# Four feed-forward blocks computed ahead instead of five, in a gated linear-attention and SwiGLU kernel, with GpSimd products, masked states by bank and another product order in two units

## The chip, the cores and the metric

The kernel runs on one core of a Trainium2 chip. The core has a matrix engine (TensorE, PE in the profile, with its weight loads shown apart as PEld), a vector engine (VectorE, DVE), a scalar engine (ScalarE, ACT), a general engine (GpSimd, POOL) and a queue engine (SyncE, SP) that here only issues transfers. The metric is the device time of one execution in microseconds (us); before the change the median of three runs is 1647.71 us (1643.01 to 1648.73).

## The reference

`x` is 2048 rows of 576. It is normalised (layer norm without weights), and two branches read the result: linear attention with 32 heads of 18, and a SwiGLU feed-forward network with 4608 hidden columns. The output is `x + s * silu(ffn)`.

```python
def _A_ref(x, wqkv, w_phi, wo):
    qkv = (x @ wqkv).reshape(B, S, 3, H, Dh)              # q, k, v by head
    pq = jnp.einsum("bhsd,hdf->bhsf", q, w_phi)           # pk likewise
    phi_q = concat([softmax(pq), softmax(-pq)])           # phi_k likewise: 36 features a head
    kv = jnp.einsum("bhsf,bhsd->bhfd", phi_k, v)
    z  = jnp.einsum("bhsf->bhf", phi_k)
    num = jnp.einsum("bhqf,bhfd->bhqd", phi_q, kv)
    den = jnp.einsum("bhqf,bhf->bhq", phi_q, z)[..., None] + 1e-6
    return (num / den).reshape(B, S, D) @ wo
def _B_ref(x, w_gate, w_up, w_down):
    return (silu(x @ w_gate) * (x @ w_up)) @ w_down
```

## The kernel before

Every float32 operand of a large product is split into a high and a low part, and three products (high by high, high by low, low by high) are added in PSUM. The rows of `x`, normalised and transposed, lie in eight tiles `X00` to `X13`: two row halves, four column blocks of 128 plus a packed remainder.

**Order of the program.** First a preparation (norm, folding of `w_phi` into the key and query weights), then the key stage, which adds up the 36 by 18 state of each head and the key sums in the PSUM tiles `kvp`. At its end the states are masked to block diagonals and split into `KVH` and `KVL`, and the key sums go through `zc` and two small products into `zb`, where every partition holds all of them. Then comes the query stage, then the feed-forward stage, twice over the 36 blocks of 128 hidden columns: once per row half.

**Query stage.** It goes over 16 row tiles (`q_tile`), in eight pairs. A tile is 28 matmuls of 288 columns into the PSUM tile `p2` (one buffer), two maxima and subtractions on VectorE, two exponentials on ScalarE into `e`, a sum per head (`sm`), the product of `e` with the key sums (`ez`), its sum per head (`y`), reciprocals, and the scaling of `e`. For each pair `numer` transposes `e` (`pt`), splits it (`ph`, `pl`), multiplies by the states (`po`), splits again (`oh`, `ol`), and `project` multiplies by the output weights and copies out (`so`).

**Blocks ahead.** While the query stage waits for VectorE and ScalarE, TensorE works on the first EARLY feed-forward blocks in the plain way (`early_tile`): for each row half two tiles, each 14 matmuls of 512 columns for the gate and 14 for the up projection, into two PSUM banks `pe`. ScalarE takes the SiLU, VectorE multiplies, and the result `h` goes to `h_dram`. The last such block (EARLY - 1) is written behind the query stage: its first row half, then the loads of the operand tiles of the feed-forward stage (`operands`, the sums of `x` blocks that the key stage stored in `sum_dram`), then its second row half.

**Feed-forward stage.** A block that was not computed ahead is a unit of `gate_up`: gate and up for 1024 rows by a Winograd form of Strassen's product, seven products of seven matmuls of 512 columns in the PSUM tiles `px` (two buffers), `py` and `pw`, with ScalarE copies (`snap`) and VectorE additions between them. Its weights (`gate_up_weights`) are loaded (`ld`), combined on GpSimd (`ts`, `ld`), split (`w`), and stored in `w_dram` for the second row half. A block that was computed ahead is a unit of `stored`, which only loads `h`. The products with `w_down` run from a queue whose items `fill` puts between the products of `gate_up`; they write `pd`. `tails` prepares the remainder rows of the weights for four blocks at a time and stores them in `t_dram`.

**What sets the order.** Source order and priorities go through a scheduler that fixes the order on each engine ahead of time; `issue_after` adds an order on one engine without a wait. On the chip each engine takes its instructions in that order, and each queue its transfers: an instruction that waits holds up all behind it on its engine.

## Time and profile before

| | |
|---|---|
| median of three runs | 1647.71 us (1643.01 to 1648.73) |
| the profiled execution | 1645.38 us, span 1643.6 us |
| granted TensorE clock, mean | 0.998 |
| preparation and key stage | 0 to about 230.5 us |
| query stage, up to its first transposes | 230.5 to 271 us |
| query stage, the rest | 271 to 488 us |
| last block ahead | 488 to 512.7 us |
| feed-forward stage | 512.7 us to the end |

A busy time is the sum of an engine's instructions. Rows of a group read: line, engine, operation, tiles (out<-in), shapes, count, then busy time in us and mean length in ns of one, then the idle time of the engine just before them and what ended it. A row of the timeline reads: start, length, engine, line, operation, tiles, count, and in brackets the idle time before and who ended it. The ends of matmuls are modelled and overlap, so the pace of a run of matmuls is taken from the chain of waits, where a piece is start, length and count.

### The profile page before, as it was taken

Reading aid. Unit: us, or ns where it says so; the run is one execution under the profiler, and the core shown is the slowest. Engines: PE = TensorE matmul, PEld = TensorE weight load, DVE = VectorE, ACT = ScalarE, POOL = GpSimd, SP = SyncE. Lnnn points to the kernel's source line nnn. Section 1 sums busy time; section 2 is a strip of 40 time slices with the busy share of each in tenths; the row PEclk is TensorE's granted clock in tenths of the full one; section 3 lists DMA queues with packets and bytes.
Section 4 is the critical chain, followed back from the end, with each engine's and each line's share of the span. In section 5 each row is a group of like instructions: output and inputs, shape, how many; then the busy total and the mean of one; then the engine's idle time right before and its main releaser. Section 6 shows DMA issues by size and latency. Waiting matters only on the chain.

```text
span 1643.6 us, 25222 instructions
## 1 busy us (share of the span) xinstructions
PE 1606.3 (98%) x9385; PEld 1428.2 (87%) x9385; DVE 1173.2 (71%) x1733; ACT 723.1 (44%) x1407; POOL 655.0 (40%) x699
## 2 busy tenths in 40 slices
PE   6999999999999999999999999999999999999997
PEld 5899987999987788888888888888888888888886
DVE  7667768989862678788777788825566766666578
ACT  5533344454432554454444444445433433333334
POOL 3385661433213455355445365313243324133132
PEclk9999999999999999999999999999999999999999
DMA  9522243433239545555545554685454655555445
GB/s 293 197 79 78 88 133 114 119 109 110 79 108 329 183 162 172 182 171 177 174 167 181 178 176 156 222 299 157 134 159 138 199 183 172 168 180 182 139 114 173
DMA packets 121741, 268.47 MB, mean 163 GB/s; under 512 B 12786, under 2 KB 53362, under 8 KB 119826
## 3 DMA queue, kind: packets, MB, share of 16 engines
q1 hardware_dynamic: 106652, 246.49, 45.8%
q0 software_dynamic: 3072, 11.02, 2.5%
q10 hardware_dynamic: 11894, 9.35, 1.8%
q8 instruction: 74, 1.21, 0.3%
q14 instruction: 49, 0.40, 0.1%
HBM read 167.19 MB, written 99.61 MB: 162 GB/s over the span
## 4 chain that ended last, share of the span: by engine, by line
PE 66%; DVE 2%; DMA 1%; issue 1%; POOL 0%; ACT 0%; SPq 0%; DVEq 0%; ACTq 0%
PE pd L805 24%; PE px L706 24%; PE pw L706 12%; PE py L706 6%; PE pe L92 1%; DVE acc L777 0%; DVE w L59 0%; DMA rb<-in_B_w_down 0%; DMA ld<-in_B_w_gu 0%; DVE hh L59 0%; DMA X<-s_dram 0%; DVE dw L59 0%; DVE ha L766 0%; DVE acc L778 0%; DVE s L740 0%
## 5 line engine op out<-in xcount | busy, mean ns | idle before, releaser
L805 PEld LDWEIGHTS pd<-dw,hh 128*128 128x128 f32 x3048 | 433.6, 189 | 25.5 <-DVE dw L59 2.0
L805 PE MATMUL pd<-dw,hh 128*128 128x288 f32 x3048 | 449.7, 297 | 3.2 <-DVE dw L59 1.5
L706 PE MATMUL px<-X,w 128*128 128x512 f32 x1488 | 385.9, 393 | 2.1 <-ACT w L58 1.3
L706 PEld LDWEIGHTS px<-X,w 128*128 128x128 f32 x1488 | 270.2, 188 | 55.5 <-ACT s L735 4.0
L706 PE MATMUL pw<-X,w 128*128 128x512 f32 x744 | 191.8, 393 | 0.0
L706 PEld LDWEIGHTS pw<-X,w 128*128 128x128 f32 x744 | 139.1, 188 | 31.2 <-DVE s L740 0.3
L740 DVE TENSOR_TENSOR s<-pw,s 128x512 f32<-128x512 f32 x124 | 85.3, 688 | 103.2 <-ACT s L735 91.7
L930 DVE TENSOR_TENSOR acc<-pd,acc 128x576 f32<-128x576 f32 x128 | 96.3, 753 | 85.3 <-PE pd L805 85.1
L735 ACT COPY s<-px 128x512 f32<-128x512 f32 x124 | 72.6, 586 | 160.0 <-PE px L706 159.9
L92 PE MATMUL pe<-X,wh 128*128 128x512 f32 (+1 forms) x380 | 121.4, 401 | 5.3 <-ACT h L119 2.2
L58 ACT CAST hh<-ha 128x512 fp32r<-128x512 f32 x140 | 82.7, 619 | 92.9 <-PE pd L805 72.6
L59 DVE TENSOR_TENSOR hh<-ha,hh 128x512 fp32r<-128x512 f32 x140 | 109.9, 811 | 18.1 <-ACT hh L58 17.1
L902 POOL TENSOR_TENSOR hb<-hb 128x512 f32<-128x512 f32 x34 | 46.7, 1372 | 161.9 <-DVE hb L762 161.5
L59 DVE TENSOR_TENSOR w<-ld,w 128x512 fp32r<-128x512 f32 (+1 forms) x93 | 79.6, 858 | 37.6 <-ACT w L58 36.3
L706 PE MATMUL py<-X,w 128*128 128x512 f32 x372 | 97.7, 396 | 1.1 <-ACT py L747 1.1
L706 PE MATMUL px<-X,wt 96*128 96x512 f32 x248 | 97.9, 395 | 0.0
L915 POOL TENSOR_TENSOR ha<-ha 128x512 f32<-128x512 f32 x34 | 52.6, 1563 | 104.0 <-DVE hh L59 104.0
L889 POOL TENSOR_TENSOR h<-ha,hb 128x512 f32<-128x512 f32 x34 | 44.9, 1321 | 123.2 <-DVE ha L766 90.1
L58 ACT CAST w<-ld 128x512 fp32r<-128x512 f32 (+1 forms) x93 | 50.9, 549 | 90.1 <-POOL ld L696 58.0
L92 PEld LDWEIGHTS pe<-X,wh 128*128 128x128 f32 (+1 forms) x380 | 69.9, 189 | 20.6 <-DVE h L122 3.4
L693 POOL TENSOR_TENSOR ts<-ld 128x256 f32<-128x256 f32 x31 | 27.3, 880 | 140.7 <-issue 70.0
L747 ACT COPY py<-px 128x512 f32<-128x512 f32 x62 | 35.5, 572 | 103.7 <-PE px L706 84.4
(262 smaller groups left out, 3238.1 us busy)
## 6 DMA issues: line engine op xcount, KB each, us to landing
w_dram<-w SPq DMA_DIRECT2D x90, 512.0 KB, 2.9
w<-w_dram SPq DMA_DIRECT2D x90, 512.0 KB, 4.5
wt<-t_dram SPq DMA_DIRECT2D x61, 336.0 KB, 3.6
ld<-in_B_w_gu SPq DMA_DIRECT2D x31, 512.0 KB, 4.5
X<-sum_dram SPq DMA_DIRECT2D x8, 1280.0 KB, 11.4
rt<-in_B_w_down SPq DMA_DIRECT2D x33, 288.0 KB, 3.0
rb<-in_B_w_down SPq DMA_DIRECT2D x33, 288.0 KB, 4.3
w_dram<-w SPq DMA_DIRECT2D x30, 256.0 KB, 2.2
```

The source lines that it names most:

```text
L58: nc.scalar.copy(hi, src)
L59: nc.vector.tensor_sub(lo, src, hi)
L92: last = nc.tensor.matmul(ps, l, r, start=n == 0, stop=n == len(pairs) - 1)
L706: nc.tensor.matmul(ps, l, r, start=first and n == 0, stop=last and n == len(mm) - 1, skip_group_check=True)
L735: nc.scalar.copy(t, ps)
L740: nc.vector.tensor_add(t, ps, t)
L747: nc.scalar.copy(yp, xp)
L805: nc.tensor.matmul(ps, l, r, start=first and n == 0 and m == 0, stop=n == len(hs) - 1 and m == 2, skip_group_check=True)
L889: sub(s, g["h"][0][0], g["h"][0][1])
L902: nc.gpsimd.tensor_add(a21, a21, g["h"][1][1])
L915: sub(a12, a12, g["h"][0][0])
L930: nc.vector.tensor_add(a2, pd[:, :, 0:HALF], a2)
```

## The change

- EARLY is 4: the plain way takes four blocks, and `gate_up` 32 units in each row half instead of 31. TAILS stays 8.
- Each row tile's product with the key sums moves from VectorE (one of 1152 elements) to GpSimd (two of 576), each with its own sum on VectorE. The buffer `ez` becomes two of half the size.
- In `tails` the subtraction of 896 elements moves from VectorE to GpSimd, and eight of the twelve stores from the GpSimd queue to SP. Both groups of GpSimd instructions are put behind the key-sum products of given row tiles.
- Masking and splitting of the states go by PSUM bank (three steps instead of ten), the key sums are copied out by bank, and `zb` is filled by two copies instead of four.
- In the first two units of `gate_up` the products run in another order, the one with S4 into a free `pd` bank, and no `fill` is called. `operands` loads in a matching order.
- The last `so` copies get high priority.

```diff
-EARLY = 5
+EARLY = 4
...
-            for i in range(3):
-                for j in range(4 if i < 2 else 2):
-                    w = GROUPS[(4 * i + j) // 2][1]
-                    nc.scalar.copy(zc[0:w, 4 * i + j:4 * i + j + 1], kvp[i][0:w, j, w:w + 1])
...
+            banks = [(i, 4 if i < 2 else 2, GROUPS[2 * i][1]) for i in range(3)]
+            for i, n, w in banks:
+                nc.scalar.copy(zc[0:w, 4 * i:4 * i + n], kvp[i][0:w, 0:n, w])
...
+            nc.scalar.copy(z2[:, :, 0:o], zp[:, :, 0:o])
+            nc.scalar.copy(z2[:, :, o:D], zq[:, 0:2 * (D - o)].rearrange("p (s n) -> p s n", s=2))
+            for i, n, w in banks:
+                km = qc.tile([GW, 4, GW], F32, name="km")
+                nc.vector.tensor_mul(km[0:w, 0:n, 0:w], kvp[i][0:w, 0:n, 0:w],
+                                     m4[0:w, 0:w].unsqueeze(1).to_broadcast([w, n, w]))
+                split(KVH[0:w, 4 * i:4 * i + n, 0:w], KVL[0:w, 4 * i:4 * i + n, 0:w], km[0:w, 0:n, 0:w])
...
-            def tails(n):
+            def tails(n, k):
...
+                with tc.issue_after(sums_z[2 * k + 1].ins):
+                    sub(t[:, 4], t[:, 2], t[:, 0])
...
                 nc.scalar.copy(hi, t)
-                nc.vector.tensor_sub(t, t, hi)
...
-                        nc.gpsimd.dma_start(t_dram[n, q, b], src[32 * q:32 * q + 32])
+                with tc.issue_after(sums_z[2 * k + 3].ins):
+                    sub(t, t, hi)
+                    for b, src in enumerate((hi.bitcast(F32), hi.bitcast(F32), t)):
+                        for q in range(4):
+                            (nc.sync, nc.sync, nc.gpsimd)[b].dma_start(t_dram[n, q, b], src[32 * q:32 * q + 32])
...
-                ez = qk.tile([P, 2 * D], F32, name="ez", bufs=1)
-                nc.vector.tensor_mul(ez, e, zb)
...
-                nc.vector.reduce_sum(y, heads(ez), axis=AX.X)
+                for s in range(2):
+                    ez = qk.tile([P, D], F32, name="ez", bufs=2)
+                    sums_z.append(nc.gpsimd.tensor_mul(ez, e[:, s * D:(s + 1) * D], zb[:, s * D:(s + 1) * D]))
+                    nc.vector.reduce_sum(y[:, s * H:(s + 1) * H], heads(ez), axis=AX.X)
...
-                        nc.scalar.copy(so, ps[:, 0:HALF])
+                        with tc.high_priority() if last else ExitStack():
+                            nc.scalar.copy(so, ps[:, 0:HALF])
...
-        for n in (0, 6, 1, 3, 5, 2, 4):
+        for n in (0, 6, 3, 1, 5, 4, 2):
...
         product(wp, w, 4, S1, True, False)
+        if opening < 2:
+            product(xp, w, 5, S2, False, False)
+            s2 = snap(xp)
+            product(yp, w, 1, A12, False, True)
+            silu_y()
+            product(xp, w, 2, S3, False, False)
+            s3 = snap(xp)
+            add(wp, s3)
+            add(wp, s2)
+            zp = fps.tile([P, 2, 512], F32, name="pd", bufs=2)[:, 0]
+            product(zp, w, 3, S4, True, True)
+            add(zp, s2)
+            top(s2)
+            product(xp, w, 6, A22, False, True)
+            silu_x(s3)
+            return h
```

Three places show how it moves instructions. The first is SP's queue at the end of the query stage, where `X` are the operand tiles of the feed-forward stage, `ld` and `wt` its first weights and `h` results of the last block ahead. Before:

```order
L675 DMA ld<-in_B_w_gu 128x4x256
L691 DMA wt<-t_dram 96x896
L686 DMA w_dram<-w_5380 128x1024
L686 DMA w_dram<-w_5389 128x1024
L686 DMA w_dram<-w_5393 128x1024
L998 DMA acc<-in_B_w_down 128x576 x2
L123 DMA h_dram<-h 128x512
L662 DMA X_5302<-sum_dram 128x2560
L662 DMA X_5300<-sum_dram 128x2560
L123 DMA h_dram<-h 128x512
L662 DMA X_5304<-sum_dram 128x2560
L662 DMA X_5306<-sum_dram 128x2560
```

and with the change:

```order
L123 DMA h_dram<-h 128x512
L664 DMA X_5161<-sum_dram 128x2560
L664 DMA X_5165<-sum_dram 128x2560
L123 DMA h_dram<-h 128x512
L664 DMA X_5163<-sum_dram 128x2560
L664 DMA X_5159<-sum_dram 128x2560
L123 DMA h_dram<-h 128x512
L677 DMA ld<-in_B_w_gu 128x4x256
L693 DMA wt<-t_dram 96x896
L677 DMA ld<-in_B_w_gu 128x4x256
```

The four operand tiles now stand ahead of the first weights, and the weights behind two more results `h`.

The second place is TensorE at the entry of the feed-forward stage; `X_60`, `X_61` and `X_63` are rows of `x`, the others of the sums, and a new `w` number is another weight tile. Before:

```order
L744 MATMUL py<-X_60,w_5380 128x512
L706 MATMUL px<-X_60,w_5380 128x512 x6
L706 MATMUL px<-X_60,wt 128x512
L706 MATMUL pw<-X_5300,w_5389 128x512 x6
L706 MATMUL pw<-X_5300,wt 128x512
L706 MATMUL py<-X_61,w_5380 128x512 x6
L706 MATMUL py<-X_61,wt 128x512
L706 MATMUL px<-X_5302,w_5389 128x512 x6
L706 MATMUL px<-X_5302,wt 128x512
L706 MATMUL px<-X_60,w_5413 128x512 x5
L706 MATMUL px<-X_5304,w_5393 128x512 x6
L706 MATMUL px<-X_5304,wt 128x512
```

and with the change:

```order
L746 MATMUL py<-X_60,w_5239 128x512
L708 MATMUL px<-X_60,w_5239 128x512 x6
L708 MATMUL px<-X_60,wt 128x512
L708 MATMUL pw<-X_5159,w_5248 128x512 x6
L708 MATMUL pw<-X_5159,wt 128x512
L708 MATMUL px<-X_5161,w_5248 128x512 x6
L708 MATMUL px<-X_5161,wt 128x512
L708 MATMUL py<-X_61,w_5239 128x512 x6
L708 MATMUL py<-X_61,wt 128x512
L708 MATMUL px<-X_5163,w_5252 128x512 x6
L708 MATMUL px<-X_5163,wt 128x512
L708 MATMUL pd<-X_5165,w_5252 128x512 x6
```

Between two products into `px` there now stands one into `pw`, `py` or `pd`; before, `px` followed `px`, and the next unit's first product was cut up to stand between.

The third place is GpSimd in the query stage. Before, it prepared the remainder rows (`tl`, `th`) and issued their stores:

```order
L555 DMA t_dram<-th 32x896 x8
L555 DMA t_dram<-tl 32x896 x4
L555 DMA t_dram<-th 32x896 x8
L555 DMA t_dram<-tl 32x896 x4
L547 TENSOR_TENSOR tl<-tl 128x128
L548 TENSOR_TENSOR tl<-tl 128x128
L549 TENSOR_TENSOR tl<-tl 128x128
L550 TENSOR_TENSOR tl<-tl 128x128
```

and with the change:

```order
L571 TENSOR_TENSOR ez<-e,zb 128x576 x2
L553 TENSOR_TENSOR tl<-tl,th 128x896
L547 TENSOR_TENSOR tl<-tl 128x128
L556 DMA t_dram<-tl 32x896 x4
L548 TENSOR_TENSOR tl<-tl 128x128
L549 TENSOR_TENSOR tl<-tl 128x128
L550 TENSOR_TENSOR tl<-tl 128x128
L571 TENSOR_TENSOR ez<-e,zb 128x576 x2
L553 TENSOR_TENSOR tl<-tl,th 128x896
L556 DMA t_dram<-tl 32x896 x4
```

The products `ez` stand between the parts of the remainder rows, and the stores of `th` have gone to SP.

On TensorE, the matmuls into `pe` from the first query tile on stood as 104 ahead of the first transposes, 212 from there to the last output projection, and 104 behind it; with the change they stand as 61, 198 and 49.

More of the change, by code (lines that the diff above doesn't have):

```diff
@@ L510, in gated_hedgehog_kernel @@
-            for i in range(2 * NG):
-                o, w = GROUPS[i // 2]
-                km = qc.tile([GW, GW], F32, name="km", bufs=2)
-                nc.vector.tensor_mul(km[0:w, 0:w], kvp[i // 4][0:w, i % 4, 0:w],
-                                     mask.rearrange("p h d -> p (h d)")[0:w, 0:w])
-                split(KVH[0:w, i, 0:w], KVL[0:w, i, 0:w], km[0:w, 0:w])
+            zc = qc.tile([GW, 12], F32, name="zc")
+            m4 = mask.rearrange("p h d -> p (h d)")
+            banks = [(i, 4 if i < 2 else 2, GROUPS[2 * i][1]) for i in range(3)]
@@ new lines, in gated_hedgehog_kernel @@
+            for i, n, w in banks:
+                nc.scalar.copy(zc[0:w, 4 * i:4 * i + n], kvp[i][0:w, 0:n, w])
+            zp, zq = kps.tile([P, 2, 512], F32, name="p2"), kps.tile([P, 512], F32, name="vw")
+            for g, (o, w) in enumerate(GROUPS):
+                for s in range(2):
+                    d = zp[:, s, o:o + w] if g < NG - 1 else zq[:, s * w:s * w + w]
+                    nc.tensor.matmul(d, zc[0:w, 2 * g + s:2 * g + s + 1].to_broadcast([w, P]), ident[0:w, 0:w],
+                                     start=True, stop=True)
@@ L576, in q_tile @@
                                      den.unsqueeze(1).to_broadcast([P, 2, H]))
-                last_e.append(nc.vector.tensor_mul(heads(e), heads(e), spread(r, 2 * H)))
+                nc.vector.tensor_mul(heads(e), heads(e), spread(r, 2 * H))
                 return e
```

50 lines of the change are left out of this document (22 added, 28 removed).

## The prediction

> **What bounds the kernel now.** I read the page's engine shares and chain first, then the chain's pieces for the pace of matmuls, then the stretches around the query stage.
>
> ```profile
> PE 1606.3 (98%) x9385; PEld 1428.2 (87%) x9385; DVE 1173.2 (71%) x1733; ACT 723.1 (44%) x1407; POOL 655.0 (40%) x699
> PE 66%; DVE 2%; DMA 1%; issue 1%; POOL 0%; ACT 0%; SPq 0%; DVEq 0%; ACTq 0%
> ```
>
> TensorE is busy 98% of the span, and the chain runs through it: time is won by fewer matmuls, or where TensorE still waits. Pieces of the chain give the pace:
>
> ```profile
> 496.22 16.63 PE pe L92 x70
> 1017.33 3.22 PE pd L805 x24
> 1125.09 1.63 PE py L706 x7
> ```
>
> A matmul of 512 columns costs 237.6 ns in a plain block (16.63 / 70) and 232.9 ns in a unit (1.63 / 7), one of 288 columns 134 ns. The stretches (length, then busy time and count of PE, PEld, DVE, ACT, POOL, then granted clock, DMA share, GB/s) and, below them, the same for instructions on `pe` (there PE, PEld, DVE, ACT):
>
> ```profile
> 230.50:271.00 40.50, 36.32 (x189) 30.58 (x189) 30.80 (x52) 21.06 (x30) 15.76 (x24) 1.00 0.49 154
> 271.00:488.00 217.00, 215.66 (x1457) 196.41 (x1458) 185.68 (x288) 95.01 (x169) 58.58 (x116) 1.00 0.33 98
> 488.00:512.70 24.70, 24.61 (x107) 19.53 (x106) 5.73 (x8) 5.40 (x11) 6.42 (x8) 1.00 0.92 341
> 512.70:552.00 39.30, 35.19 (x143) 26.77 (x142) 19.93 (x26) 15.54 (x31) 16.37 (x17) 0.96 0.68 231
> ...
> 271.00:488.00 217.00, 61.36 (x213) 37.01 (x214) 5.54 (x8) 4.19 (x7) 1.00 0.33 98
> ```
>
> From 271 to 488 us TensorE idles 1.3 us while VectorE is 86% busy: the plain blocks fill what the query stage leaves open. TensorE idles 4.2 us at the stage's start and 4.1 us at the feed-forward entry. Who ended these waits (total, times, longest):
>
> ```profile
> PE pe L92 <- ACT h L119: 2.2, 2, 1.3
> PE pe L92 <- DVE h L122: 2.0, 2, 1.7
> PE pd L805 <- DVE dw L59: 1.5, 1, 1.5
> PE px L706 <- ACT w L58: 1.3, 2, 0.8
> PE p L614 <- ACT so L618: 1.3, 1, 1.3
> PE pt L588 <- DVE e L577: 1.3, 1, 1.3
> PE p L92 <- ACT zb L509: 1.1, 1, 1.1
> PE py L706 <- ACT py L747: 1.1, 2, 0.6
> PE px L706 <- ACT s L735: 0.7, 2, 0.5
> ```
>
> **The exchange of a block.** A plain block is 2 row halves x 2 tiles x 28 = 112 matmuls: 112 x 0.2376 = 26.6 us less. Two units are 2 x 7 x 7 = 98: 98 x 0.2329 = 22.8 us more, as the stage behind 552 us has TensorE full. Net -3.8 us, if what the block covered stays covered. It goes from three places: 43 matmuls (10.2 us) ahead of the first transposes, 14 (3.3 us) in the stage's body, 55 (13.1 us) behind it.
>
> **The stage's body.** TensorE's work there falls to 217.0 - 1.3 - 3.3 = 212.4 us, so VectorE must stay below that. What leaves and stays on it:
>
> ```profile
> L577 DVE TENSOR_TENSOR e<-e,sm 128x1152 f32<-128x1152 f32 x15 | 20.3, 1355 | 0.3
> L278 DVE TENSOR_REDUCE m<-p 128x32 f32<-128x576 f32 x27 | 19.9, 738 | 0.2 <-PE p L92 0.2
> L285 DVE TENSOR_REDUCE sm<-e 128x64 f32<-128x1152 f32 x14 | 18.9, 1347 | 3.8 <-ACT e L282 3.8
> L568 DVE TENSOR_TENSOR ez<-e,zb 128x1152 f32<-128x1152 f32 x14 | 18.6, 1328 | 0.0
> L570 DVE TENSOR_REDUCE y<-ez 128x64 f32<-128x1152 f32 x14 | 18.4, 1317 | 0.0
> ...
> L552 DVE TENSOR_TENSOR tl<-tl,th 128x896 f32<-128x896 f32 x8 | 8.6, 1080 | 0.0
> ```
>
> The key-sum products (18.6) and remainder subtractions (8.6) go; two half sums for one cost 14 x (2 x 0.738 - 1.317) = 2.2: 185.7 - 18.6 - 8.6 + 2.2 = 160.7 us. GpSimd at work slows VectorE where it reads two tiles from SBUF; the key stage shows that, with GpSimd's own price under contention:
>
> ```profile
> L409 DVE TENSOR_TENSOR phi<-phi,sm 128x1152 f32<-128x1152 f32 x14 | 21.7, 1548 | 0.5
> ...
> L328 POOL TENSOR_TENSOR slo<-sraw,shi 128x512 fp32r<-128x512 f32 x14 | 25.2, 1797 | 1.1
> ...
> L889 POOL TENSOR_TENSOR h<-ha,hb 128x512 f32<-128x512 f32 x34 | 44.9, 1321 | 123.2 <-DVE ha L766 90.1
> L555 POOL DMA_DIRECT2D t_dram<-tl x32 | 15.8, 499 | 82.1 <-DVE tl L552 41.8 <-DVE y L571 40.2
> ```
>
> 1548 against 1355 ns adds 15 x 0.19 = 2.9 us: VectorE has 164 of 212 us, 48 to spare, 3.0 us a row tile. A product of 576 costs GpSimd 1.49 to 2.02 us (1321 and 1797 x 576 / 512); I take 1.6. It starts behind the first exponential, so the first half sum finds it done behind VectorE's 1.35 us sum, and the second waits under 1 us: inside the 3.0. GpSimd's own load (32 x 1.6 = 51 us, subtractions 8 x 2.5, 32 stores of 0.5) is under half the stage. The body costs nothing more; queued behind a waiting half sum stand the next tile's maxima and the splits of `numer`, covered by `pe`.
>
> **The stage's start.** `zb` is filled by two copies instead of four with up to four splits between, so the 1.1 us wait falls to some 0.4: -0.7 (0 to -1.1). With 61 instead of 104 matmuls ahead of the transposes, TensorE asks for them after 84 x 0.134 + 61 x 0.2376 = 25.7 us instead of 36.0. The third row tile cannot start before VectorE has subtracted the second tile's maxima (one buffer `p2`), and VectorE's row now puts two half sums, a reciprocal and a split between them. Following that row with the lengths above, I find the third tile 2.7 us late and the transposes 0.7: 3.4 us of waits against 4.2, so -0.8 (-4.2 if all go, +4.2 if they double).
>
> **The last copies.** The 1.3 us wait for `so` had a weight cast ahead of the copy, held up by its load:
>
> ```profile
> 484.91 0.62 ACT L58 CAST w<-ld 128x512 fp32r<-128x512 f32 x1 [3.39 <-DMA ld<-in_B_w_gu]
> 485.43 0.39 ACT L618 COPY so<-p 128x288 f32<-128x288 f32 x1
> 488.37 0.40 ACT L618 COPY so<-p 128x288 f32<-128x288 f32 x1 [2.55 <-DMA s_dram<-so]
> 489.40 0.62 ACT L58 CAST w<-ts 128x512 fp32r<-128x512 f32 x1 [0.64 <-ACT so L618]
> ...
> 495.14 0.42 DVE L59 TENSOR_TENSOR w<-ld,w 128x256 fp32r<-128x256 f32 x1 [1.76 <-ACT w L58]
> 495.48 0.68 DVE L122 TENSOR_TENSOR h<-pe,h 128x512 f32<-128x512 f32 x1
> ```
>
> The copy now stands ahead of that cast: -1.3 (0 to -1.3).
>
> **Behind the stage.** 49 matmuls, 11.6 us, must cover what 104 covered. The last block's `h` stands on VectorE behind the split of the second unit's last weight tile; the last two rows above show it, 10.6 us after the first weights landed. Some 2.5 us of that the cast of `ts` stood behind the `so` copies, which now come first. So 8.1 us remain, with `h` itself 8.8, and TensorE can issue 35 matmuls (8.3 us) before it needs that bank: it waits 0.5 us longer than the first weights land behind the stage's last matmul. In SP's queue:
>
> ```profile
> 479.72 0.58 SPq L675 DMA_DIRECT2D ld<-in_B_w_gu  x1
> ...
> 496.61 3.49 SPq L662 DMA_DIRECT2D X<-sum_dram  x2
> ...
> X<-sum_dram SPq DMA_DIRECT2D x8, 1280.0 KB, 11.4
> ```
>
> They were issued 8.3 us before that matmul (488.0) and landed 5.2 us later. Now two operand tiles stand ahead of them, free some 9 us before the end: 2.6 MB at 341 GB/s take 7.7 us, then the weights 2.5: landed 1.2 us behind the end, so +1.7 us (0, if the transfers share the engines; +5, if they take the operand tiles' 11.4 us).
>
> **The entry.** The same operand tiles loaded from 496.6 us, against the first units' weights; now they are in SBUF. The new order puts another product between a copy (`s`, `py`) and the product that needs it, 1.63 us for a copy of 0.6. I take the waits for `s`, `py` and `w` as gone: -0.7 - 1.1 - 1.3 = -3.1. The wait for `dw` stays: with the third unit the queue of `w_down` products begins as before.
>
> ```profile
> 541.00:546.00 5.00, 3.58 (x13) 2.29 (x13) 4.97 (x6) 2.94 (x6) 3.53 (x3) 1.00 0.50 174
> 546.00:551.00 5.00, 4.31 (x17) 3.99 (x18) 4.16 (x7) 0.61 (x2) 2.26 (x3) 0.66 0.14 52
> ```
>
> After these waits the granted clock was 0.66 over 5 us, 1.7 us lost; I leave it in, as its last wait stays (bounds 0 and -5.8: all 4.1 and the clock). The Trainium skill (TensorE: Matmul & The Clock Gate, "What's actually happening") has the clock fall only after about 3.4 us of idleness; here it fell after waits of 0.5 and 1.5 us, so the trace differs. By the rule, shorter waits here would win no clock.
>
> **The sum.** -3.8 - 0.7 - 0.8 - 1.3 + 1.7 - 3.1 = -8.0 us. On the profiled execution's own time, 1645.4, that is 1637.4, and I say **1637**. That execution lies 2.3 us under the median of the runs shown, inside their spread. The gains' far ends give 1645.4 - 3.8 - 1.1 - 4.2 - 1.3 - 5.8 = 1629.2, the losses' 1645.4 - 3.8 + 4.2 + 5 = 1650.8.
>
> **Rivals.** *The exchange alone*: the waits at start and entry come back elsewhere, as the scheduler's order was made without the chip's times. For it: VectorE was 99% busy in 541 to 546, and splits and `dw` stay. Against: operand tiles no longer load then. 1645.4 - 3.8 + 1.7 = 1643.
>
> *A long wait behind the stage*: the weights land 11.4 us after their issue, TensorE idles 5 us, and the clock falls as at 546 (1.7 us): 1637.4 - 1.7 + 6.7 = 1642. For it: in the trace `h` came just in time with twice the cover.
>
> *Slower: the half sums wait for GpSimd*, in order, behind the remainder rows. At contended prices the products take 2 x 2.02 us, and in half the tiles a subtraction (3.1), four stores (2.0) and four short subtractions (2.1) may stand ahead, 3.6 on average: 7.6, less the 2.0 us of exponential and sum: 5.6 us a tile. Up to 3.0 is covered; the other 2.6 x 16 give 1637 + 42 = 1679. It decides from 4.1 us a tile, where 16 x 1.1 us use up the forecast's gain and put the time over 1647.7 by half a per cent. Against: at 1.6 us I find under 1. The Trainium skill (GPSIMD Engine Reference, "Key points") speaks for this rival: GpSimd is about half as fast elementwise, and the two engines contend where VectorE has two SBUF inputs. The 1548 ns row agrees; by it the price is the 2.9 us already counted.
>
> **How the numbers follow.** Forecast 56%, exchange alone 23%, long wait 12%, GpSimd 9%. A measurement here can tell about 0.5%, 8.2 us: faster means under 1639.5, slower over 1655.9. Nine tenths of the forecast's chance lie under 1639.5: faster 0.51. The rest of it and the first two rivals are no change: 0.39. GpSimd's case and mishaps: slower 0.10. The range takes in the bounds: 1629 to 1651; the forecast's own is 1630 to 1641.
>
> **What would show it.** TensorE's count on `px`, `py`, `pw` up by 98 less what went to `pd`, on `pe` down by 112; the first transposes some 12 us earlier; no waits for `s` and `py` at the entry; VectorE at 75 to 80% in the body, with waits of `y` for `ez` under 1 us; the transfer share behind the stage under 0.92. Waits of `y` over 3 us a tile, TensorE idle over 4 us ahead of the first unit, or new waits in its second and third unit would prove me wrong.

## The result, and the profile after

The changed kernel takes 1653.95 us (median of 6 runs, 1652.51 to 1656.24) against 1643.25 us for the kernel before, run beside it (6 runs, 1642.82 to 1648.73): a ratio of 1.0057, with a 95% interval of 1.0044 to 1.0070. It is slower, by 9.4 us (0.0057 x 1644), and lies above the predicted range. The medians stand 10.7 us apart, since the kernel before has runs at 1643 and at 1648; the ratio takes in all runs, and times between kernels below are differences of ratios times 1644 us. Its profiled execution took 1652.65 us, with a span of 1650.9.

The page of the changed kernel, engine shares and the chain:

```profile
PE 1606.0 (97%) x9371; PEld 1429.1 (87%) x9371; DVE 1159.5 (70%) x1717; ACT 723.2 (44%) x1397; POOL 694.9 (42%) x679
PE 67%; DVE 1%; DMA 1%; issue 0%; ACT 0%; SPq 0%; POOL 0%; ACTq 0%; DVEq 0%; POOLq 0%
```

TensorE has 14 matmuls less (9385 before), as the exchange of 112 for 98 says, and is busy as long as before, in a span 7.3 us longer. So the time is in waits, or in slower matmuls. The stretches of the program (columns as in the prediction), and below them the plain blocks' matmuls inside the second one:

```profile
229.30:261.25 31.95, 28.29 (x147) 25.18 (x147) 22.71 (x33) 15.38 (x20) 14.10 (x12) 0.89 0.47 155
261.25:487.60 226.35, 215.79 (x1444) 195.22 (x1443) 173.53 (x282) 95.34 (x169) 92.68 (x102) 0.99 0.38 113
487.60:502.80 15.20, 11.98 (x51) 9.06 (x50) 5.44 (x7) 4.69 (x10) 8.86 (x10) 1.00 0.72 249
502.80:542.00 39.20, 36.05 (x164) 28.86 (x163) 24.78 (x33) 19.16 (x39) 19.46 (x20) 1.00 0.71 245
...
261.25:487.60 226.35, 57.34 (x200) 35.37 (x200) 4.80 (x7) 4.19 (x7) 0.99 0.38 113
```

Each stretch against the same one before, in us. "Matmuls" is what the prediction's counts and prices give for the matmuls that left or came; "left over" is the rest, and "forecast" what the prediction had put there.

| stretch | before | after | change | matmuls | left over | forecast |
|---|---|---|---|---|---|---|
| up to the query stage | 230.5 | 229.3 | -1.2 | 0 | -1.2 | -0.7 |
| stage start to first transposes | 40.5 | 31.95 | -8.6 | -10.2 | +1.6 | -0.8 |
| body of the stage | 217.0 | 226.35 | +9.4 | -3.3 | **+12.7** | -1.3 |
| behind the stage | 24.7 | 15.2 | -9.5 | -13.1 | +3.6 | +1.7 |
| feed-forward to the end | 1130.9 | 1148.1 | +17.2 | +22.8 | -5.6 | -3.1 |

The body, where only the last copies had been counted (-1.3), holds 12.7 us that were not foreseen: TensorE idles 10.6 us there instead of 1.3 (9.2 us more), and its matmuls take 3.4 us longer than their counts say. The waits of TensorE, whole span, cut to those around the query stage (total, times, longest):

```profile
PE pt L590 <- DVE e L579: 5.4, 6, 2.3
PE p L92 <- DVE e L279: 3.7, 1, 3.7
PE pe L92 <- ACT h L119: 2.6, 3, 1.3
PE p L616 <- ACT so L621: 2.3, 2, 1.5
PE pe L92 <- DVE h L122: 2.2, 2, 1.9
...
PE po L596 <- ACT ph L58: 2.0, 1, 2.0
```

The waits for `e` (1.3 us before), for `so` (1.3, and at another place) and for `ph` (none) are new ones inside the body, up to 2.3 us each. The same view for the other engines, 230 to 500 us, and below it the row for `th` in the kernel before:

```profile
POOL ez L571 <- ACT e L282: 114.9, 26, 15.9
ACT th L551 <- POOL tl L550: 22.8, 6, 8.9
DVE pl L59 <- ACT ph L58: 18.1, 18, 4.0
...
DVE y L572 <- POOL ez L571: 5.4, 7, 1.4
```

```profile
ACT th L551 <- POOL tl L550: 1.5, 1, 1.5
```

The half sums `y` hardly wait for GpSimd (5.4 us in 7 waits), as forecast. It is ScalarE that waits: its cast `th` of a remainder row stands up to 8.9 us for GpSimd's differences `tl`. How one such place looks in the timeline, GpSimd first, then VectorE, then TensorE (in each row start, length, operation, and in brackets the wait):

```profile
373.41 1.43 POOL L571 TENSOR_TENSOR ez<-e,zb 128x576 f32<-128x576 f32 x1
374.79 0.46 POOL L548 TENSOR_TENSOR tl<-tl 128x128 f32<-128x128 f32 x1
375.21 0.46 POOL L549 TENSOR_TENSOR tl<-tl 128x128 f32<-128x128 f32 x1
375.74 1.47 POOL L550 TENSOR_TENSOR tl<-tl 128x128 f32<-128x128 f32 x1
378.26 2.11 POOL L553 TENSOR_TENSOR tl<-tl,th 128x896 f32<-128x896 f32 x1 [1.05 <-ACT th L551]
...
373.78 3.11 DVE L579 TENSOR_TENSOR e<-e,sm 128x1152 f32<-128x1152 f32 x1
379.30 1.16 DVE L573 TENSOR_TENSOR y<-y,sm 128x64 f32<-128x64 f32 x1
381.36 1.36 DVE L579 TENSOR_TENSOR e<-e,sm 128x1152 f32<-128x1152 f32 x1
...
382.78 1.54 PE L590 MATMUL pt<-ident,e 128*126 128x128 f32 x6 [2.33 <-DVE e L579]
```

While GpSimd works from 373.4 to 377.2, VectorE's scaling of `e` takes 3.11 us instead of 1.36; while GpSimd subtracts from 378.3 to 380.4, the little product `y` takes 1.16 us, where its mean before was 0.22 (over the whole body 0.48 now). Together 2.7 us, and the next `e` is late by what TensorE then waits, 2.3 us. Two other places go through ScalarE's order. The first pair of rows is ScalarE at 348, the second ScalarE behind the stage:

```profile
348.29 0.94 ACT L551 CAST th<-tl 128x896 fp32r<-128x896 f32 x1 [3.42 <-POOL tl L550]
349.13 0.39 ACT L621 COPY so<-p 128x288 f32<-128x288 f32 x1
...
489.36 0.40 ACT L621 COPY so<-p 128x288 f32<-128x288 f32 x1 [3.94 <-DMA s_dram<-so]
491.49 0.62 ACT L58 CAST w<-ld 128x512 fp32r<-128x512 f32 x1 [1.73 <-DMA s_dram<-so]
```

At 348 the copy `so` stands behind `th`, and TensorE waits 1.5 us for it. At 489 the copy waits 3.9 us for the store of the buffer it reuses, and the casts of the first weights and of `h` stand behind it: the two waits of `pe` for `h`.

This left three theories. **A**: the remainder rows, bound on GpSimd between the key-sum products, make ScalarE wait. **B**: the key-sum products on GpSimd cost by themselves. **C**: the block is missed as cover. A fourth, **D**, says that GpSimd's company slows VectorE, whoever waits; **E** and **F** came up later.

### The profile page after: what moved, and what is told of

Same layout as the page of the kernel before. It is cut to its first block, busy times and chain, and to the rows that moved or that the text cites. A ratio compares the mean times of both kernels' runs of the same rounds, so it can differ in the third digit from the quotient of the medians.

```text
span 1650.9 us, 25208 instructions
## 1 busy us (share of the span) xinstructions
PE 1606.0 (97%) x9371; PEld 1429.1 (87%) x9371; DVE 1159.5 (70%) x1717; ACT 723.2 (44%) x1397; POOL 694.9 (42%) x679
## 4 chain that ended last, share of the span: by engine, by line
PE 67%; DVE 1%; DMA 1%; issue 0%; ACT 0%; SPq 0%; POOL 0%; ACTq 0%; DVEq 0%; POOLq 0%
PE px L708 25%; PE pd L833 24%; PE pw L708 12%; PE py L708 6%; DVE acc L805 0%; DVE hh L59 0%; DMA rb<-in_B_w_down 0%; DMA X<-s_dram 0%; DVE w L59 0%; ACT w L58 0%; DVE acc L806 0%; SPq L891 0%; PE pd L708 0%; DVE s L742 0%; DVE acc L988 0%
## 5 line engine op out<-in xcount | busy, mean ns | idle before, releaser
L708 PE MATMUL px<-X,w 128*128 128x512 f32 x1536 | 396.9, 393 | 1.1 <-ACT s L737 1.1
L708 PEld LDWEIGHTS px<-X,w 128*128 128x128 f32 x1536 | 279.3, 188 | 55.6 <-ACT s L737 4.1
L92 PE MATMUL pe<-X,wh 128*128 128x512 f32 x300 | 97.7, 402 | 5.8 <-ACT h L119 2.6
L571 POOL TENSOR_TENSOR ez<-e,zb 128x576 f32<-128x576 f32 x32 | 49.4, 1544 | 121.9 <-ACT e L282 114.9
L708 PEld LDWEIGHTS py<-X,w 128*128 128x128 f32 x384 | 68.8, 188 | 11.5
```

Source lines behind the costliest of these rows:

```text
L92: last = nc.tensor.matmul(ps, l, r, start=n == 0, stop=n == len(pairs) - 1)
L571: sums_z.append(nc.gpsimd.tensor_mul(ez, e[:, s * D:(s + 1) * D], zb[:, s * D:(s + 1) * D]))
L708: nc.tensor.matmul(ps, l, r, start=first and n == 0, stop=last and n == len(mm) - 1, skip_group_check=True)
```

## First experiments: parts undone, and the exchange alone

**Remainder rows as before, the rest as changed.**

```diff
-                with tc.issue_after(sums_z[2 * k + 1].ins):
-                    sub(t[:, 4], t[:, 2], t[:, 0])
...
-                    sub(t, t, hi)
+                nc.vector.tensor_sub(t, t, hi)
...
+                with tc.issue_after(last_e[3 * n // 2 + 2].ins):
+                    tails(n)
```

> The changed kernel, with only the remainder rows done as before: released by the last product of a query tile, their low part by VectorE, all twelve stores on GpSimd's queue. Theory A (GpSimd takes the remainder rows' differences and low part in its order behind the key-sum products, ScalarE's in-order cast th stands up to 8.9 us for them, and the twelve us of new TensorE gaps in the query stage follow from it): the wait of th for tl falls from 22.8 us to some 2, the gaps of TensorE in the body from 12 to under 4, the time from 1654 to 1643 to 1646. Theory B (the key-sum product on GpSimd is itself the late link, half by half): no change beyond 2 us, 1652 to 1656. Theory C (one block less to fill with is the loss): no change, 1652 to 1656.

Measured: 1649.78 us, ratio 1.0035 (1.0023 to 1.0047). The wait of `th` falls from 22.8 to 4.3 us and the gaps of the body (starts of neighbouring matmuls compared with their usual pace, gaps over 0.4 us added up, from the first transposes to the first matmul behind the last projection) from 12.0 to 4.3, as A said, but of the 9.4 us only 3.6 come back. The third tile's scores wait longer at the stage's start, 5.9 us, and there are 2.3 us of a new wait in the first unit.

**Key-sum product back on VectorE too.**

```diff
-                    sums_z.append(nc.gpsimd.tensor_mul(ez, e[:, s * D:(s + 1) * D], zb[:, s * D:(s + 1) * D]))
+                nc.vector.tensor_mul(ez, e, zb)
```

> The changed kernel with the remainder rows as before and the key-sum product on VectorE as before, one of 1152 columns: nothing of the query stage is on GpSimd that was not there before; four blocks ahead, the masked states by bank and the new product order stay. Theory A: like the run with the remainder rows alone undone, within 2 us (1643 to 1646), or a little slower for the 3 us a tile that VectorE gets back. Theory B: the gaps of the body go only here, 1640 to 1645, while the run before it stays at 1654. Theory C: still 1650 to 1655, since the block is still gone.

Measured: 1651.84 us, ratio 1.0046 (1.0034 to 1.0058). Neither A nor B: with four blocks the old query stage is no better than the new one.

**Five blocks, the rest as changed** (`EARLY = 5`).

> The changed kernel with five blocks ahead as before, all else as changed. Theories A and B: the gaps in the query stage stay (10 to 13 us), the FFN is 17 us shorter and the stage with what lies behind it 26.6 us longer less the 3.5 us of waits there that the fifth block fills: 1654 to 1661. Theory C: the time of before comes back, 1641 to 1646.

Measured: 1652.11 us, ratio 1.0052 (1.0040 to 1.0063). Not C: the block comes back, the time of before does not. Gaps of the body 12.4 us.

**The kernel before with four blocks** (`EARLY = 4`).

> The kernel before with four blocks ahead and nothing else of the change. Theories A and B (the exchange of a block in itself gains its 3.8 us of matmuls, and may lose some of it to waits behind the stage): 1639 to 1645. Theory C: 1649 to 1656, with gaps of TensorE in the body or behind it of ten us and more.

Measured: 1654.21 us, ratio 1.0057 (1.0045 to 1.0070), with 12.0 us of gaps in the body, 4.0 of them right at its end, ahead of the first unit: C as well. So the exchange alone loses all that the whole change loses, and the rest alone loses nearly as much; together they lose it only once. Two causes were at work, and had to be taken apart at a fixed number of blocks.

## The query stage at five blocks

Three kernels with five blocks complete a square with the third run above. The first has both edits shown above (remainder rows and key-sum product as before), the second the one of the remainder rows alone, the third the one of the key-sum product alone:

```diff
-EARLY = 4
+EARLY = 5
```

> Five blocks ahead, remainder rows and key-sum product as before: of the change only the masked states by bank, the priority of the last copies and the new product order in two FFN units are left. The run with five blocks and the rest as changed had a body of 227.5 us with 12.4 us of gaps, and an FFN of 1119.6 us against 1123.8 before. If the two GpSimd parts are the whole loss of the body: body back at 216 to 218 with under 3 us of gaps, FFN 1119 to 1121, time 1638 to 1641, below before. If the states by bank or the copies' priority cost something too: 1643 or more.

> Five blocks ahead, remainder rows as before, the key-sum product halves on GpSimd as changed. Theory A (the loss comes from the remainder rows' place on GpSimd): gaps of the body 12.4 to about 4, body 218 to 220, some 3 to 6 us left at the stage's start, time 1642 to 1646 against 1652 with both. Theory B (the product halves are the loss): 1650 to 1653.

> Five blocks ahead, key-sum product on VectorE as before, the remainder rows on GpSimd bound to it as changed: nothing stands between the four differences of a row on GpSimd any more. If the interleaving of the two is what makes ScalarE wait, the wait of th for tl falls under 5 us and the body's gaps under 4, time 1639 to 1643. If the remainder rows cost by their place alone (bound a tile or two later, stores on SyncE's queue), the gaps stay at 8 us or more, 1647 to 1652.

| five blocks | product on VectorE | product on GpSimd |
|---|---|---|
| remainder rows as before | 1638.77 us, 0.9965 (0.9952 to 0.9979) | 1648.64 us, 1.0029 (1.0016 to 1.0042) |
| remainder rows on GpSimd | 1639.49 us, 0.9974 (0.9965 to 0.9982) | 1652.11 us, 1.0052 (1.0040 to 1.0063) |

The columns are 10.5 us (0.0064 x 1644) and 12.8 us apart, the rows 1.5 and 3.8. The product on GpSimd costs in both rows. The remainder rows on GpSimd add 1.5 us on the left, which is inside the noise, and 3.8 on the right, just outside it. The body in the four corners, product on VectorE first, and the remainder rows as before first in each pair:

```profile
272.20:489.20 217.00, 215.82 (x1457) 196.64 (x1458) 185.56 (x288) 95.57 (x170) 57.85 (x116) 1.00 0.32 97
```

```profile
269.50:489.10 219.60, 217.89 (x1467) 198.81 (x1468) 179.50 (x282) 93.66 (x168) 39.07 (x54) 1.00 0.29 90
```

```profile
263.40:482.40 219.00, 214.72 (x1444) 194.28 (x1443) 179.96 (x294) 94.92 (x170) 104.37 (x147) 1.00 0.35 97
```

```profile
262.50:490.00 227.50, 216.85 (x1444) 195.53 (x1443) 177.01 (x286) 96.58 (x171) 97.37 (x105) 0.99 0.33 97
```

With the product on VectorE TensorE idles 1.2 and 1.7 us, although VectorE is busy for 186 of 217 us; with it on GpSimd 4.3 and 10.7 us, at 177 to 180 us of VectorE. The second pair also has 13 to 23 matmuls less to do. Less work on VectorE, and more waits.

The upper right corner, 1648.64 us, fits neither forecast. A's body came (gaps from 12.4 to 5.1 us, 227.5 to 219.0 us) and its time did not: a new wait stands ahead of the first transposes. GpSimd, then VectorE, in that run:

```profile
248.75 0.46 POOL L546 TENSOR_TENSOR tl<-tl 128x128 f32<-128x128 f32 x1 [7.46 <-DMA h_dram<-h]
250.65 1.40 POOL L569 TENSOR_TENSOR ez<-e,zb 128x576 f32<-128x576 f32 x1
252.09 0.75 DVE L570 TENSOR_REDUCE y<-ez 128x32 f32<-128x576 f32 x1 [5.76 <-POOL ez L569]
```

Between the first tile's two half products GpSimd has the differences of a remainder row, and stands 7.5 us for a transfer. (The profile names another store of that queue; in the run with four blocks and a third `so` buffer, further down, the same row waits 7.68 us for the row's own load, `tl<-in_B_w_tail`.) The second half product comes behind them, `y` waits 5.8 us for it, and TensorE 6.4 us for the third tile's scores.

Against the upper left corner, with the plain matmuls that moved taken out, some 4 of the 10.5 us lie there and some 5 in the body. So the remainder rows were in the products' way in both rows, only at another place. No run has the products on GpSimd and the rows off it, so what the products cost alone is not shown. Nor was TensorE's order held: with the product on GpSimd and rows as before, its plain matmuls stand as 61, 199 and 160 (ahead of the first transposes, in the body, behind), against 104, 213 and 103.

**The cast one tile later.** Meant to take ScalarE's wait away and leave all else:

```diff
-                nc.scalar.copy(hi, t)
                 with tc.issue_after(sums_z[2 * k + 3].ins):
+                    nc.scalar.copy(hi, t)
+                with tc.issue_after(sums_z[2 * k + 5].ins):
                     sub(t, t, hi)
```

> The changed kernel, with ScalarE's cast th of a remainder row released one query tile later (by the product that releases the low part so far), and the low part another tile later; engines, counts and queues as changed. Theory A (ScalarE stands in its order at th for GpSimd's differences, and copies of so and ph stand behind it): the wait of th for tl falls from 22.8 us to under 5, the gaps of TensorE in the body from 12 to 5 to 8, the time from 1654 to 1647 to 1651. Theory D (GpSimd's work itself slows VectorE: rows of 1.34 us that took 3.11, of 0.24 that took 1.2, while GpSimd worked): the wait of th goes but the gaps stay above 9 us, 1652 to 1656.

Measured: 1658.38 us, ratio 1.0085 (1.0071 to 1.0099). It failed as a test: the cast still waits for the differences, and now also for the low part of the row before, since `th` is a single buffer.

```profile
ACT th L552 <- POOL tl L550: 15.8, 4, 8.9
ACT th L552 <- POOL tl L554: 12.3, 4, 3.6
```

**The start.** In the changed kernel one of the two `ez` buffers holds rows of `wo` while the first tile runs.

```diff
-                   qk.tile([P, D], F32, name="ez", bufs=2).unsqueeze(1)]
+                   qk.tile([P, 2, D], F32, name="e", bufs=4)]
```

> Five blocks ahead, remainder rows as before, key-sum halves on GpSimd; new: the last rows of wo, which lie in one of the two ez buffers until their split, lie in one of the four e buffers, so the first tile has both halves of ez. The run without this had 6.6 us of gaps ahead of the first transposes and 5.1 us in the body, at 1648.6. Theory E (the loss sits at the stage's start, where the second half product of the first tile waits for the first half's sum because the other buffer is taken): the gap of 6.5 us at the third tile's scores falls under 3 us, time 1641 to 1645. Theory B (it sits in each tile's chain through GpSimd): 1647 to 1650.

Measured: 1652.14 us, ratio 1.0047 (1.0034 to 1.0061). The gap ahead of the third tile fell from 6.5 to 3.1 us, but the scheduler made another order of it (230 plain matmuls in the body instead of 199, 7.4 us of work) and the body took 11 us more. So the run says that the start is not the whole loss, and no more. In the run without this edit the buffer was not what ended last: `y` of the first half was done at 245.3 us, and the second half product ran at 250.65, behind the remainder row shown above.

**Products that nobody waits for.** To the old query stage with five blocks are added, per tile:

```diff
+                for s in range(4):
+                    dz = qk.tile([P, HALF], F32, name="dz", bufs=1)
+                    c = slice(s * HALF, (s + 1) * HALF)
+                    nc.gpsimd.tensor_mul(dz, e[:, c], zb[:, c])
```

> Five blocks ahead, remainder rows and key-sum product as before (1638.8), and on top four GpSimd products of 288 columns a query tile, after the tile's last product, whose result nobody reads: the same 1152 columns a tile as the moved product, with no one waiting for them. Theory D (GpSimd's products slow VectorE's rows beside them, and that makes the loss): VectorE's rows of 1.35 us lengthen as in the change (mean 1.6 of the normalization), body 221 us or more, time 1643 to 1648. If it is the waits for the products that cost, not their company: 1638 to 1641.

Measured: 1642.83 us, ratio 0.9997 (0.9988 to 1.0006), 5.3 us (0.0032 x 1644) above the same kernel without them. The order on TensorE has the same counts, and nobody reads the result. VectorE's rows without them, then with them:

```profile
L279 DVE TENSOR_TENSOR e<-p,m 128x576 f32<-128x576 f32 x28 | 20.9, 745 | 0.1
L285 DVE TENSOR_REDUCE sm<-e 128x64 f32<-128x1152 f32 x14 | 18.9, 1347 | 3.8 <-ACT e L282 3.8
L567 DVE TENSOR_TENSOR ez<-e,zb 128x1152 f32<-128x1152 f32 x14 | 18.6, 1329 | 0.0
```

```profile
L567 DVE TENSOR_TENSOR ez<-e,zb 128x1152 f32<-128x1152 f32 x14 | 23.3, 1663 | 0.0
...
L279 DVE TENSOR_TENSOR e<-p,m 128x576 f32<-128x576 f32 x28 | 20.8, 744 | 0.1
...
L285 DVE TENSOR_REDUCE sm<-e 128x64 f32<-128x1152 f32 x14 | 18.9, 1347 | 3.6 <-ACT e L282 3.6
```

VectorE's product of two tiles from SBUF goes from 1329 to 1663 ns beside GpSimd; the row that reads PSUM (744) and the sum with one input (1347) do not move. The expectation named the scaling of `e`; here it was `ez` that met GpSimd, so the mechanism is D's, at another row. The body took 219.9 us, 2.9 more than without them, where D had 221 or more, and the time lies just under D's range. The Trainium skill (GPSIMD Engine Reference, "Key points") says that the two engines contend where VectorE has two SBUF inputs; these rows agree. Company thus gives about half of the 10.5 us, with some 2.7 us of noise either way. These products take somewhat more of GpSimd's time than the moved ones (four of 0.92 us a tile against two of 1.55), so half is rather too much than too little. The other half would then go with the waits for GpSimd and with the other order on TensorE; this is what is left over, and was not tried by itself.

## The exchange of the block

**The new order in two units alone**, in the kernel before (the branch for the two units as the change has it, and the order of the loads):

```diff
-        for n in (0, 6, 1, 3, 5, 2, 4):
+        for n in (0, 6, 3, 1, 5, 4, 2):
...
+        if opening < 2:
+            product(xp, w, 5, S2, False, False)
```

> The kernel before with the new order of products in the two first FFN units, and of the operands' loads, alone. The prediction gave these 3.1 us; with five blocks and the rest of the change the FFN was 4.2 to 5.9 us shorter than before. Expected from that: 1638 to 1641, FFN 1118 to 1121. If states by bank or the copies' priority made the gain: 1643.

Measured: 1640.75 us, ratio 0.9978 (0.9969 to 0.9987): 3.6 us less, where the prediction had 3.1. The length of its feed-forward stage alone is not known.

**What four blocks lack.** In the run with four blocks and the old query stage TensorE stops for a copy that stops for a store (SP's queue, ScalarE, TensorE):

```profile
426.85 4.15 SPq L663 DMA_DIRECT2D X<-sum_dram  x2
...
427.66 0.33 ACTq L620 DMA_DIRECT2D s_dram<-so  x1
...
437.60 0.40 ACT L619 COPY so<-p 128x288 f32<-128x288 f32 x1 [4.69 <-DMA s_dram<-so]
...
438.05 0.61 PE L614 MATMUL p<-WOH,oh 126*128 126x288 f32 x1 [4.64 <-ACT so L619]
```

The copy at 437.60 reuses the buffer whose store was issued at 427.66, so that store took some 10 us. Beside it run two operand tiles of the feed-forward stage, 1280 KB each. With five blocks the last block ahead still reads the buffers they go to, and they load behind the stage (from 496.6 us before the change); with four the last block is done earlier, and the loads are issued at 426.85. The transfer share from 430 to 440 us is 0.81, where the run with five blocks has 0.40. The row in that run, ScalarE at the same copy, has no such wait:

```profile
433.97 0.40 ACT L619 COPY so<-p 128x288 f32<-128x288 f32 x1 [0.50 <-PE p L614]
```

A third buffer takes the copy's wait away and leaves the transfers where they are:

```diff
-                        so = qk.tile([P, HALF], F32, name="so", bufs=2)
+                        so = qk.tile([P, HALF], F32, name="so", bufs=3)
```

> Four blocks ahead, remainder rows and key-sum product as before (1651.8, against 1638.8 with five blocks), and a third buffer for the projected rows so. Theory F (with the fifth block gone nothing is left to run while a copy so waits for the store of the buffer it reuses: 4.7 us at 433, 2.2 and 1.2 us at the end, and half clock behind both): these waits go, the gaps of the body fall from 11.5 to under 5, the first unit starts 5 to 10 us earlier, time 1640 to 1645. Theory C (the fifth block covered the weights' way into the FFN): the body's gap goes but the first unit waits for weights as long, 1647 to 1651.

Measured: 1640.97 us, ratio 0.9979 (0.9970 to 0.9989), 11.0 us below the same kernel with two buffers; gaps of the body from 11.5 to 2.9 us, the first unit at 488.3 instead of 498.3 us. Theory F holds in its wait; what it said of work that is left to run beside it is not needed, since the loads moved into the stage lengthen the store. That these loads are the reason is read from the trace and was not tried by itself. Is this also what the changed kernel suffers from? Four more kernels have the third buffer: the changed one with that edit alone; with the remainder rows as before; with five blocks and both parts as before; and with the key-sum product as before.

> The changed kernel with a third so buffer and nothing else. Theory F (the body's loss is the wait of a copy for the store of its buffer, as it was with four blocks and the old query stage, where the third buffer gave 10.9 us): 1642 to 1647. Theory B (the key-sum products on GpSimd make the loss, and their own early blocks left behind the stage cover its end already): gaps of the body stay at 8 us or more, 1649 to 1654.

> The changed kernel with remainder rows as before (1649.8) and a third so buffer: of the change's query stage only the key-sum halves on GpSimd are left. Theory F: 1640 to 1645. Theory B: 1646 to 1651, some 5 to 10 us above the run with the product on VectorE too (1641.0).

> Five blocks ahead, remainder rows and key-sum product as before (1638.8), and a third so buffer. Theory F: the fifth block covered these waits, so nothing changes, 1637 to 1640, and against 1641.0 with four blocks the exchange of a block is worth 0 to minus 3 us, not the 3.8 us of gain that its matmuls promise. If the third buffer is worth something by itself: under 1636.

> The changed kernel with the key-sum product on VectorE as before and a third so buffer: all of the change but that product. Theory B (that product is the one part of the query stage that costs): 1639 to 1643, 11 to 14 us below the changed kernel. If the remainder rows on GpSimd cost by themselves: 1645 and more.

| third `so` buffer | product on VectorE | product on GpSimd |
|---|---|---|
| five blocks, rows as before | 1637.18 us, 0.9956 (0.9943 to 0.9969) | |
| four blocks, rows as before | 1640.97 us, 0.9979 (0.9970 to 0.9989) | 1651.40 us, 1.0040 (1.0024 to 1.0056) |
| four blocks, rows on GpSimd | 1644.12 us, 0.9992 (0.9984 to 1.0001) | 1650.76 us, 1.0035 (1.0021 to 1.0048) |

In the changed kernel the third buffer gives 3.6 us only (1.0057 to 1.0035, some 3 either way). What it took away lies behind the stage, where the 15.2 us shrink to 11.9 and TensorE hardly waits:

```profile
488.60:500.50 11.90, 11.54 (x49) 8.99 (x49) 5.28 (x7) 3.86 (x8) 8.63 (x10) 1.00 0.91 322
```

The body keeps its gaps, 13.0 us. Taking back the key-sum product besides brings 7.1 us (10.0 in the row above, with the remainder rows as before) and the body with it, by these rows (product on GpSimd, then on VectorE):

```profile
259.30:488.60 229.30, 217.76 (x1444) 196.81 (x1443) 174.79 (x284) 96.12 (x171) 93.76 (x103) 0.99 0.37 112
```

```profile
271.10:490.70 219.60, 216.44 (x1452) 196.26 (x1452) 178.50 (x279) 95.25 (x170) 39.08 (x54) 1.00 0.35 109
```

The last corner, 1644.12, lies above the 1639 to 1643 expected, so the remainder rows on GpSimd may cost some 2 us here (0.0013 x 1644; the intervals of the two runs overlap). With the product on GpSimd their price is 3.8 us at five blocks and none that can be seen at four with the third buffer; beside that product it stays open.

And the exchange itself, with the `so` wait out of the way: 0.9956 with five, 0.9979 with four, a loss of 3.8 us (the intervals just part) instead of a gain of 3.8. The missing 7.6 us lie largely in the entry: from the first unit to the end it takes 1152.4 us with four blocks and 1124.4 with five, 28.0 more where two units add 22.8. The 22 us from 523 us with four blocks, and a stretch at the same distance from the first unit with five:

```profile
523.00:545.00 22.00, 18.89 (x84) 16.12 (x83) 12.03 (x19) 12.02 (x25) 9.26 (x10) 0.84 0.52 185
```

```profile
546.00:568.00 22.00, 21.79 (x117) 18.90 (x117) 14.64 (x21) 13.94 (x28) 11.99 (x12) 1.00 0.61 213
```

84 matmuls against 117, with a wait of 3.1 us and at a clock of 0.84:

```profile
526.74 2.92 PE L707 MATMUL px<-X,w 128*128 128x512 f32 x6 [3.11 <-ACT s L736]
```

The copy `s` stood on ScalarE behind casts of weights, and these waited for GpSimd's combinations (0.7 and 1.4 us). Without 24 us of plain matmuls behind the query stage, the first units start with nothing ahead of the work that feeds them; this is read from the trace, not tried.

**The best version** found is the one with five blocks, the query stage as before, the masked states by bank, the new order in two units and the third `so` buffer: 1637.18 us, 0.9956 of the kernel before (0.9943 to 0.9969), better than both. It is not told apart from the same with two `so` buffers (0.9965).

## Why the prediction was wrong

Adding the parts one after the other, each by its difference of ratios times 1644 us. A step is good to some 2 to 3 us, so the second and the last are not told from nothing:

| step | ratio | us |
|---|---|---|
| kernel before, with the new product order | 0.9978 | -3.6 |
| and states by bank, priority of the last copies | 0.9965 | -2.1 |
| and the key-sum product on GpSimd | 1.0029 | **+10.5** |
| and the remainder rows on GpSimd | 1.0052 | +3.8 |
| and four blocks for five | 1.0057 | +0.8 |

- **The step that failed is "The body costs nothing more".** It compared VectorE's 164 busy us with 212 and spread the 48 to spare evenly, 3.0 us a tile. Nearly all that this argument foresaw came true: VectorE was busy 173.5 of 226.35 us (77%, forecast 75 to 80), and `y` waited 5.4 us in 7 waits for `ez`, under 1 us each on average. But VectorE had 9.5 us more to do than the 164 forecast, and the body was 12.7 us longer than its matmuls all the same. In four pairs of runs that differ in the key-sum product alone, the one with it on GpSimd is 7 to 13 us longer. TensorE's order is fixed, so a result that is late at one place stops it there, and plain matmuls that stand elsewhere do not fill the hole.
- **Company was counted on the wrong account.** The prediction saw VectorE's rows slowed beside GpSimd (1548 against 1355 ns), priced it at 2.9 us and charged it to the spare time. The rows did lengthen, the scaling of `e` to a mean of 1610 ns (15 x 0.255 = 3.8 us more), and the little product `y`, which was not counted, from 0.22 to 0.48 (3.9 us more); but products that no one waited for cost 5.3 us of the kernel's time (2.9 of it seen in the body). Rows that TensorE waits for have no spare time.
- **The slower rival had the right place and, in the changed kernel, the wrong engine.** It put the remainder rows and the products into each other's way on GpSimd, and so they are; but it let VectorE's `y` wait in every tile, 42 us in all. In the changed kernel what waited was ScalarE's cast `th`, with `so` and `ph` behind it; `y` waited long once, 5.8 us at the stage's start, where the remainder rows were done as before. That GpSimd also reads the products late (114.9 us of waiting for `e`), and holds the differences meanwhile, was not followed.
- **The exchange** was right in its matmuls (14 less) and wrong in its cover. In the changed kernel it is worth +0.8 us, give or take 3, instead of the -2.1 that the term and its +1.7 behind the stage made. The prediction saw the operand tiles move ahead and asked only whether the weights behind them land in time; the wait came from the `so` copy, whose store runs beside them, with the weights' casts behind it, and the third buffer took it away (the 3.6 us above). With the old query stage the same wait is clear of noise, 11.0 us.
- **The entry** came as forecast: -3.1, and -3.6 for the new order alone. In the changed kernel the waits for `py` and `w` are gone, those for `s` are not (1.1 us, against 0.7), and `dw` has 2.0. The stage's left over, -5.6, is 2.5 us better than forecast; the fall of the clock, which the prediction left in (1.7 us), is part of it: 1.00 from 502.8 to 542 us where it was 0.96.
- **The start**: first transposes 9.8 us earlier (271.0 to 261.25) where 12 were forecast. The wait for the third tile's scores was 3.7 us instead of 2.7, and the clock fell behind it.

None of the signs that the prediction named for being wrong would have caught the body: its list watched VectorE, the first unit and the entry, and not ScalarE.

## What to carry to other kernels

Work that is moved off a busy engine is to be judged by who waits for its result and what stands behind that waiter, not by the spare time of either engine: here VectorE lost 18.6 us of work in the body and the kernel 10. Filler work does not only fill the holes that the profile shows; it also holds back transfers that wait for its buffers, so before taking some away look at what will load earlier, and beside which stores (here two of 1280 KB beside a copy with two buffers). And when two undone parts each fail to bring the time back, hold one fixed and test the other at both values: the four corners told in one round with which part the loss comes and goes, what four single reversals had not. Even so, a part that is put back brings its own waits along, so look where the time of each corner lies before its difference is read as a price.

## What the runs showed of the hardware

- Two waits of 3 to 4 us cost TensorE some 3 us each besides, since the granted clock behind them was 0.50 for about 6 us: behind the 3.1 us in the 22 us shown above, and behind the 3.7 us for the third tile in the changed kernel. The changed kernel, then the run with four blocks, each behind its wait:

```profile
253.80:259.40 5.60, 5.60 (x24) 5.60 (x25) 5.33 (x8) 2.21 (x3) 1.46 (x1) 0.50 0.34 115
526.80:532.90 6.10, 6.10 (x20) 5.42 (x21) 2.54 (x5) 2.19 (x5) 0.75 (x1) 0.50 0.84 281
```

- VectorE and GpSimd can slow each other by far more than a mean shows where they meet: 3.11 us for a row of 1.36, and 1.47 us for a GpSimd row of 0.46, in the same 2 us.
- The store of a copy of 144 KB took some 10 us beside two loads of 1280 KB, though the median of these stores from issue to landing in that run was 2.2 us.
